# Where the right-hand stack of SBUF tiles begins: an edge of 480 bytes in place of 96, and two constant tiles in the other order

## The chip, the core and the metric

The kernel runs on one core of a Trainium2 chip. The metric is the device time of one execution in microseconds (us), as the median of several runs; smaller is better. The engines are named as the profile names them: PE is TensorE's matrix multiply, PEld its weight load, DVE is VectorE, ACT is ScalarE, POOL is GpSimd and SP is SyncE, which issues the DMA transfers.

## What is computed

Three stages follow each other, all in float32. The first is a chunked linear attention with decay over 4 batches of 8 heads, 768 positions, head size 32 and state size 16. Its result, 3072 tokens of 256 features, passes through two feed-forward layers.

```python
x = attn_out.transpose(0, 2, 1, 3).reshape(B * S, H * D)   # 3072 x 256
h = x @ w_in                                               # 256 -> 2048
g = where(h > 0, h, exp(min(h, 0)) - 1)
x = g @ w_out                                              # 2048 -> 256
g = x @ w_gate; val = x @ w_val                            # 256 -> 1536, twice
out = (g * sigmoid(g) * val) @ w_out2                      # 1536 -> 256
```

## The kernel before

Tokens are worked on in 6 blocks of 512. Features lie on the 128 partitions and the 512 tokens of a block on the free axis, so that a large matmul has a weight of 128x128 as its stationary operand and 128x512 as its moving one. To keep float32 precision with the cheaper type float32r, every operand is split into a high and a low part, and a product is made of three matmuls: high by high, low weight by high, high weight by low (`mm3`, L485 to L493, and `m_c`, L527).

Two feed-forward phases follow each other. In the first, `seq1` runs over 6 blocks of 16 feature tiles f, and one slot of it is `m_a` (6 matmuls that write `h`, L506) and, three slots late, `m_c` (6 matmuls that write `c`, L541). Block 0 is different: its `c` is made by plain float32 matmuls (L535). The attention of the next block's four units is spread among the slots of the current block, so the attention's small matmuls and its work on DVE, ACT and POOL lie beside the feed-forward matmuls. In the second phase a slot (b, f), with 6 blocks of 12 feature tiles, is `s_a` (6 matmuls that write `g` and 6 that write `v`) and, three slots late, `s_c` (6 that write `o`). Each engine runs its instructions in the order in which the program issues them; `m_end` (L544 to L547) empties the accumulators `c` at the end of a block on ACT and DVE.

SBUF is filled from two sides. Tile pools without a side are stacked from low addresses up (the left stack), pools with `side="right"` are stacked from the top of the memory down (the right stack). Each partition's top is at byte 229,344, which is 447 times 512 and 480 more. The right stack begins with a tile named `edge` that nothing reads or writes; after it come `w1p` (the first phase's weights, w1h and w1l), `xp` (its inputs xh and xl), and `stage` (raw weights, e, v). Every tile of the right stack has a size that is a multiple of 512 bytes. With an edge of 24 floats, 96 bytes, every right tile therefore begins 384 bytes past a multiple of 512. On the left, the constant tiles come first: `ident8` (4096 bytes) at byte 16,512, which is 128 past a multiple of 512, then `con` (1408 bytes), also at 128 past one, then `zero_q` (512 bytes) at a multiple of 512. After these `x2` and all further left tiles that a matmul reads begin at a multiple of 512: the split results gh and gl (pool `work`), and in the second phase part of the weights and inputs.

In the second phase the tiles are divided between the two sides by two lines: the weights w2h and w2l of tile f are in the left stack for f below 4 and in the right stack from 4 on, and the block's inputs x2h and x2l are in the left stack for even blocks and in the right one for odd blocks.

```python
pool = ph2["w2l" if f < NHL else "w2h"]      # pair_w2: w2h, w2l (NHL = 4)
pool = ph2["xs" if b % 2 == 0 else "w2h"]    # s_x: x2h, x2l
```

The lower end of the right stack, 132,992 before, lies 384 bytes above the upper end of the left one (132,608) while the attention and the `stage` pool are open.

Of the kernel before, what the change touches and what calls it, by code (L numbers as in the profile page):

```python
# [8 lines left out]
F32 = mybir.dt.float32  # L9
# [38 lines left out]
WARM = 0  # L48
LEAD = 4
CON = 352  # L50
EDGE = 24
VB = 2
OX = 13
NW = 3
# [15 lines left out]
def ssm_mlp_glu_kernel(ctx, tc, a, bcs, xbc, w1, w2, consts, out):  # L70
# [4 lines left out]
    const = ctx.enter_context(tc.tile_pool(name="const", bufs=1))  # L75
    x2p = ctx.enter_context(tc.tile_pool(name="x2p", bufs=1))
    work = ctx.enter_context(tc.tile_pool(name="work", bufs=3))

    ident8 = const.tile([128, H, Q], F32, name="ident8")
    con = const.tile([128, CON], F32, name="con")  # L80
    ident_r, ident, blk_sb, sgn_sb = (con[:, x:y] for x, y in ((0, R), (R, R + Q), (R + Q, R + 2 * Q), (R + 2 * Q, R + 2 * Q + 2)))
    zero_q = const.tile([128, Q], F32, name="zero_q")
    x2_all = x2p.tile([128, 2 * NT], F32, name="x2")
# [1 line left out]

    ctx.enter_context(tc.tile_pool(name="edge", bufs=1, side="right")).tile([128, EDGE], F32, name="edge")
    right = ExitStack()
# [744 lines left out]
```

## Time and profile before

| what | value |
|---|---|
| median of 3 runs | 654.52 us (654.43 to 654.73) |
| the profiled execution's own time | 654.61 us |
| its span, first to last instruction | 652.8 us |
| PE busy | 625.6 us, 96% of the span, 3620 matmuls |
| PEld busy | 490.4 us, 3620 weight loads |
| DVE, ACT, POOL busy | 388.1, 312.2, 315.2 us |
| mean granted TensorE clock | 1.00 of 2.4 GHz |

The span is what the profile sees; the execution's own time is longer by what lies around the first and the last instruction. Busy time of PE is the union of matmuls that overlap in their pipeline, so it says that PE had work, not how fast it went: that is read from the distance between the starts of two matmuls. In the chain of waits, a row such as "1.40 PE o L493 x6" is six matmuls in a row that nothing held up but the one before each.

### The profile page before, as it was taken

The page shows a single profiled execution, that of the slowest core. Times are in us where ns is not written, and L with a number is a line of the kernel's source. Part 1 is how long each engine was busy: PE and PEld are TensorE (multiplying, and loading weights), DVE is VectorE, ACT ScalarE, POOL GpSimd, SP SyncE. Part 2 cuts the span into 40 slices and gives each one's busy share as a digit, 9 for nine tenths or more (in the row PEclk, how much of TensorE's full clock was granted, in tenths as well). Part 3 has the DMA queues.
Part 4 walks back from the last instruction along what each step waited for, and adds up shares of the span by engine and source line. Part 5 has one row for each costly group of instructions (what it writes and reads, how often), then busy time and mean ns, then how long its engine had stood idle before and what let it go on. Part 6 is the DMA issues. An engine that isn't in the chain of part 4 may idle for free.

```text
span 652.8 us, 9659 instructions
## 1 busy us (share of the span) xinstructions
PE 625.6 (96%) x3620; PEld 490.4 (75%) x3620; DVE 388.1 (59%) x580; ACT 312.2 (48%) x562; POOL 315.2 (48%) x263
## 2 busy tenths in 40 slices
PE   2599999999999999999999999999999999999997
PEld 1356667777787778777788888888888888888886
DVE  5869987878887788783574663343343343343332
ACT  2146666666667666666775542322332232332322
POOL 2636657767777577764454332333233333333332
PEclk9999999999999999999999999999999999999999
DMA  6785634454344543410310000000000000000000
GB/s 181 200 286 192 171 111 143 126 151 144 127 133 132 149 133 122 133 33 19 95 50 0 2 1 1 33 0 1 32 1 1 33 1 0 34 0 2 32 1 32
DMA packets 21646, 49.54 MB, mean 76 GB/s; under 512 B 4320, under 2 KB 6496, under 8 KB 21600
## 3 DMA queue, kind: packets, MB, share of 16 engines
q1 hardware_dynamic: 21600, 48.93, 24.1%
q8 instruction: 28, 0.46, 0.3%
q14 instruction: 18, 0.15, 0.1%
HBM read 45.68 MB, written 3.24 MB: 75 GB/s over the span
## 4 chain that ended last, share of the span: by engine, by line
PE 87%; DVE 5%; issue 2%; DMA 2%; ACT 2%; SPq 1%; POOL 0%; POOLq 0%; DVEq 0%; ACTq 0%
PE h L493 18%; PE o L493 15%; PE g L493 15%; PE v L493 15%; PE c L541 14%; PE c L535 4%; DVE E L316 1%; DMA raw<-in_w 1%; PE cb L370 1%; PE y L446 1%; PE y L442 1%; DVE m L521 1%; DVE w2e L140 1%; DMA w2e<-in_xbc 1%; ACT m L515 1%
## 5 line engine op out<-in xcount | busy, mean ns | idle before, releaser
L499 POOL TENSOR_TENSOR gl<-m,gh 128x512 fp32r<-128x512 f32 x152 | 200.1, 1319 | 259.3 <-ACT gh L498 255.5
L613 DVE TENSOR_TENSOR m<-m,g 128x512 f32<-128x512 f32 x72 | 49.5, 688 | 168.5 <-ACT m L608 168.5
L608 ACT ACTIVATE m<-g 128x512 f32<-128x512 f32 x72 | 43.1, 598 | 190.5 <-PE g L493 190.5
L521 DVE SCALAR_TENSOR_TENSOR m<-m,h 128x512 f32<-128x512 f32 x96 | 65.6, 683 | 62.1 <-ACT m L520 62.1
L498 ACT ACTIVATE gh<-m 128x512 fp32r<-128x512 f32 x152 | 94.8, 624 | 1.6 <-DVE m L614 1.0
L515 ACT ACTIVATE m<-h 128x512 f32<-128x512 f32 x96 | 57.1, 595 | 69.1 <-PE h L493 64.5
L493 PE MATMUL h<-xh,w1h 128*128 128x512 f32 x192 | 80.6, 420 | 1.5 <-DVE xl L478 1.0
L493 PE MATMUL h<-xh,w1l 128*128 128x512 f32 x192 | 75.9, 395 | 0.0
L541 PE MATMUL c<-gh,w1h 128*128 128x512 f32 x160 | 63.8, 399 | 1.0 <-DVE x L547 1.0
L541 PE MATMUL c<-gh,w1l 128*128 128x512 f32 x160 | 62.4, 390 | 0.0
L520 ACT ACTIVATE m<-m 128x512 f32<-128x512 f32 x96 | 59.9, 623 | 0.5
L493 PE MATMUL h<-xl,w1h 128*128 128x512 f32 x192 | 59.9, 393 | 0.0
L493 PE MATMUL o<-gl,w2h 128*128 128x512 f32 x144 | 56.7, 394 | 0.0
L493 PE MATMUL g<-x2h,w2h 128*128 128x512 f32 x144 | 56.7, 394 | 0.0
L493 PE MATMUL o<-gh,w2h 128*128 128x512 f32 x144 | 56.6, 393 | 0.0
L493 PE MATMUL o<-gh,w2l 128*128 128x512 f32 x144 | 56.5, 393 | 0.0
L493 PE MATMUL v<-x2h,w2h 128*128 128x512 f32 x144 | 56.5, 392 | 0.0
L493 PE MATMUL g<-x2h,w2l 128*128 128x512 f32 x144 | 56.5, 392 | 0.0
L493 PE MATMUL v<-x2h,w2l 128*128 128x512 f32 x144 | 56.4, 392 | 0.0
L614 DVE TENSOR_TENSOR m<-m,v 128x512 f32<-128x512 f32 x72 | 49.5, 688 | 7.9 <-DVE m L613 0.5
L541 PE MATMUL c<-gl,w1h 128*128 128x512 f32 x160 | 50.4, 396 | 0.0
L493 PEld LDWEIGHTS h<-xh,w1h 128*128 128x128 f32 x192 | 36.4, 190 | 14.4 <-DVE m L521 3.5
(126 smaller groups left out, 1091.3 us busy)
## 6 DMA issues: line engine op xcount, KB each, us to landing
abc<-ac SPq DMA_DIRECT2D x16, 512.0 KB
bcraw<-in_bcs SPq DMA_DIRECT2D x32, 256.0 KB
raw<-in_w SPq DMA_DIRECT2D x15, 512.0 KB
w2e<-in_w SPq DMA_DIRECT2D x12, 512.0 KB
xb<-in_xbc SPq DMA_DIRECT2D x17, 256.0 KB
raw<-in_w SPq DMA_DIRECT2D x12, 256.0 KB
out_y<-yo SPq DMA_DIRECT2D x12, 256.0 KB
abc<-ac SPq DMA_DIRECT2D x8, 128.0 KB
```

The lines of the kernel that those rows point to most:

```text
L140: nc.vector.tensor_scalar(halves(v)[:, :, 0], t["h16"][:, :, 1], 13, None, ALU.logical_shift_right)
L493: nc.tensor.matmul(dst, lhsT=l, rhs=r, start=first and i == 0, stop=last and i == len(ops) - 1, **kw)
L498: nc.scalar.activation(hi, src, AF.Copy)
L499: lo_eng.tensor_tensor(lo, src, hi.bitcast(F32), ALU.subtract)
L515: nc.scalar.activation(m, h, AF.Relu, scale=-1.0)
L520: nc.scalar.activation(m, m, AF.Exp, scale=-1.0)
L521: nc.vector.scalar_tensor_tensor(m, m, -1.0, h, ALU.add, ALU.max)
L535: nc.tensor.matmul(cps[b][m], lhsT=W1["v", f][:, m * 128:(m + 1) * 128], rhs=g, start=f == 0, stop=f == NF1 - 1)
L541: nc.tensor.matmul(cps[b][m], lhsT=w[:, m * 128:(m + 1) * 128], rhs=r, start=f == 0 and w is wh and r is gh, stop=f == NF1 - 1 and r is gl)
L608: nc.scalar.activation(m, pg, AF.Sigmoid)
L613: nc.vector.tensor_tensor(m, m, pg, ALU.mult)
L614: nc.vector.tensor_tensor(m, m, pv, ALU.mult)
```

## The change

The edge grows from 24 to 120 floats (from 96 to 480 bytes), and `con` is allocated before `ident8`. No instruction is added, taken out or reordered.

```diff
-EDGE = 24
+EDGE = 120
...
+    con = const.tile([128, CON], F32, name="con")
     ident8 = const.tile([128, H, Q], F32, name="ident8")
-    con = const.tile([128, CON], F32, name="con")
```

All right tiles move 384 bytes down, and begin at multiples of 512; the lower end of the right stack then meets the upper end of the left one at 132,608. `con` takes byte 16,512 (128 past a multiple of 512, as before) and `ident8` moves to 17,920, a multiple of 512. `zero_q`, `x2` and the rest of the left stack stay where they are, since the sum of the constants is the same.

## Rows read from the trace of the kernel before

**Rows 1.** The page: busy time by engine, TensorE's granted clock in 40 slices, chain by engine.
```profile
PE 625.6 (96%) x3620; PEld 490.4 (75%) x3620; DVE 388.1 (59%) x580; ACT 312.2 (48%) x562; POOL 315.2 (48%) x263
PEclk9999999999999999999999999999999999999999
...
PE 87%; DVE 5%; issue 2%; DMA 2%; ACT 2%; SPq 1%; POOL 0%; POOLq 0%; DVEq 0%; ACTq 0%
```

**Rows 2.** Busy time in stretches: each engine's us and instruction count, then clock, DMA share, GB/s.
```profile
157.00:209.00 52.00, 51.43 (x334) 40.99 (x335) 42.77 (x61) 34.21 (x65) 39.87 (x32) 1.00 0.42 136
...
408.00:457.00 49.00, 49.00 (x216) 40.15 (x215) 18.10 (x26) 14.96 (x26) 14.99 (x13) 1.00 0.03 11
```

**Rows 3.** Waits of PE, from 100 to 346 us: total us, times, longest.
```profile
PE c L541 <- DVE x L547: 1.0, 3, 0.6
```

**Rows 4.** Chain of waits in block 2 of the second phase: start, us, what.
```profile
458.03 1.36 PE g L493 x6
459.39 1.36 PE v L493 x6
460.75 1.37 PE o L493 x6
462.12 1.39 PE g L493 x6
463.51 1.40 PE v L493 x6
```

**Rows 5.** The same view in block 5 of the second phase.
```profile
603.55 1.40 PE g L493 x6
...
628.34 1.38 PE g L493 x6
629.71 1.36 PE v L493 x6
```

**Rows 6.** Timeline of PE in block 4 of the second phase: start, us, instruction.
```profile
558.85 0.39 PE L493 MATMUL v<-x2h,w2h 128*128 128x512 f32 x1
```

**Rows 7.** Timeline of the weight loads at the same place.
```profile
558.85 0.19 PEld L493 LDWEIGHTS v<-x2h,w2l 128*128 128x128 f32 x1
```

**Rows 8.** Timeline of PE: the first matmul of blocks 0, 1 and 2, second phase.
```profile
345.84 0.40 PE L493 MATMUL g<-x2h,w2h 128*128 128x512 f32 x1
...
395.81 0.39 PE L493 MATMUL g<-x2h,w2h 128*128 128x512 f32 x1
...
445.45 0.40 PE L493 MATMUL g<-x2h,w2h 128*128 128x512 f32 x1
```

**Rows 9.** Chain of waits in block 5 of the first phase: one slot.
```profile
316.81 1.39 PE c L541 x6
318.20 1.38 PE h L493 x6
```

**Rows 10.** Chain of waits in block 0: plain float32 matmuls, the last of 15 rows.
```profile
98.70 1.72 PE c L535 x4
```

**Rows 11.** Chain of waits at the end of a block of the first phase: first and last piece off PE.
```profile
248.31 0.60 ACT m L515
...
261.21 0.61 DVE x L547
```

**Rows 12.** Scans on DVE, by shape: line, operation, count, busy us, mean ns.
```profile
L316 DVE TENSOR_TENSOR_SCAN E<-abc,ident 128x1024 f32<-128x1024 f32 x16 | 36.2, 2265 | 0.1
...
L316 DVE TENSOR_TENSOR_SCAN E<-abc,x 128x512 f32<-128x512 f32 x5 | 6.0, 1205 | 0.7 <-ACT x L647 0.7
...
L334 DVE TENSOR_TENSOR_SCAN P<-ahn,zero_q 128x128 f32<-128x128 f32 x14 | 5.7, 407 | 0.0
```

**Rows 13.** Chain of waits: transfers on it, into the right stack and into the left.
```profile
5.46 4.56 DMA raw<-in_w
19.60 4.23 DMA w2e<-in_xbc
...
145.37 3.78 DMA raw<-in_w
```

## The prediction

> **What bounds the kernel now.** I read the page first. PE is busy for 625.6 of 652.8 us at a granted clock that stands at the top digit in every slice, and the chain of waits lies on PE for 87% [rows 1]. So the end is set by how fast PE goes through its matmuls, and the clock has nothing left to give. The busy times by stretch say where this holds. In a block of the second phase PE is busy for all 49.00 us while DVE, ACT and POOL work 15 to 18 us; in a block of the first phase PE still has 51.43 of 52 us, but DVE has 42.77 [rows 2]. PE's own waits there are few: 1.0 us in three places, all for the DVE copy that empties an accumulator at a block's end [rows 3]. PE is thus the bound, with little slack only around those three places.
>
> Busy time doesn't tell what a matmul costs, so I next read the chain of waits for groups of six matmuls, which all have the same shape (128x128 by 128x512) and no wait among them. They don't take the same time. In block 2 of the second phase the groups g, v, o take 1.36, 1.36, 1.37 us and the next g and v 1.39 and 1.40 [rows 4]; in block 5 it goes the other way round, 1.40 for g of an early tile and 1.38 and 1.36 for g and v of a later one [rows 5]. The code says what differs. Block 2 has its inputs on the left; its weights are on the left up to f = 3, on the right after that, and the change from 1.37 to 1.39 falls on g of f = 4. Block 5 has its inputs on the right, and its rows change at f = 4 in the opposite sense. Fast are left with left and right with right; slow is one of each. Tile number, block and position in the slot are excluded by this reversal.
>
> The timelines show why two operands can meet at all: a matmul (558.85 us) and the load of the next weight (also 558.85 us) begin together, and the load runs for 0.19 us beside it [rows 6, 7]. So PE reads two tiles at once. Left tiles begin at 0 modulo 512, right ones at 384. The rows fit this reading: when the moving operand and the weight loaded beside it begin at the same place modulo 512, six matmuls take about 1.36 us (227 ns each), otherwise about 1.40 (233 ns). Whatever the reason in the memory, the rows hold at both places, 0 with 0 and 384 with 384.
>
> **The edge.** It makes all right tiles begin at 0, so every pair becomes an equal one. No queue gets or loses an instruction; what moves is the pitch of the matmuls.
>
> Second phase: blocks start at 345.84, 395.81 and 445.45 [rows 8], so an even block takes 49.97 us, an odd one 49.64; the next three repeat this within 0.02. A block is 12 slots of three groups. With three groups at 1.36, a slot is 4.08 and a block 48.96. (The run of equal pairs from 458.03 to 462.12 took 4.09 [rows 4], but beside its last matmul a right-hand weight is already loading.) The gain is 1.01 for an even block and 0.68 for an odd one, three of each: 5.1 us. At 4.09 it would be 12 x 4.09 = 49.08 a block and 4.4 us in all; I keep that as the low end.
>
> First phase: a slot is 1.39 for c (moving operand left, weights right) and 1.38 for h (both right) [rows 9], 2.77 together; 5 blocks of 16 such slots make 80. That h isn't at 1.36, although its pair is equal, needs a choice. The first g behind an unequal o is also slower than what follows it (1.38, and 1.36 for the v after it [rows 5]), so I read 1.38 as the trace of the unequal c before it: PE needs a few matmuls to fall into step. With c equal, h should fall too. The attention's small matmuls break in some four times a block, though, so I take the 4.09 of the mixed run: two thirds of it, 2.727 a slot, 0.043 less than now, times 80: 3.4 us. Ends: 2.72 a slot (4.0 us), or c falls to h's 1.38 and h stays (0.01 x 80 = 0.8 us).
>
> What is lost of it: at three block ends the chain leaves PE (from 248.31 to the end of the DVE copy at 261.82 in one of them [rows 11], 13.6 us through ACT and DVE), and PE waits for that copy already [rows 3]. A faster PE arrives earlier and waits longer. In 13.6 us at 1.6% (0.043 of 2.77) that is 0.21 us each, 0.65 for three; it is the work that is late next. Its ends are nothing lost, and all of the first phase's gain.
>
> Block 0's plain float32 matmuls are 1.72 for four in all 15 of the chain's rows, of which one is shown [rows 10], though a third of their weights lies on the right: no gain, no loss. The 45 us of start before them hang on transfers and on the attention; nothing there gets faster.
>
> **The transfers into and out of right tiles.** Their count and size stay; their start in a partition moves from 384 to 0. The trace doesn't show that case. A 512 KB load into a right tile took 4.56 us on the chain at the start, a 256 KB load into a left one 4.23, and one such right load stands on the chain again later, 3.78 us [rows 13]. The nearest bound is the whole difference of the first two, 0.33 us either way for each of the two that are on the chain. I take nothing: their times follow the queue rather than the place.
>
> **The constants' order.** `con` keeps its place modulo 512, `ident8` goes from 128 to 0. It is read only by DVE's 16 large scans. Two scans that read at 0 give a slope: (1205 - 407) / (512 - 128) = 2.078 ns per element, 141 ns fixed, thus 2269 ns for 1024 elements; those that read `ident8` at 128 take 2265 [rows 12]. The place makes 4 ns, 0.06 us over all 16, on an engine that is not the bound. I take nothing; ends are plus and minus 0.06.
>
> **The sum.** 5.1 + 3.4 - 0.65 = 7.85 us off the profiled execution's 654.61 (its span 652.8 and 1.8 around it, which the change doesn't touch): 646.8. The median of the runs is 0.09 below the profiled one, so 646.7.
>
> **A page that speaks against it.** The Trainium skill, page "SBUF — State Buffer", section "Who interferes with whom", gives PE two independent read ports, one for the moving operand and one for the weight load, and says that PE never waits on anyone. By it the place of a tile would change nothing and the time would stay at 654.5. The trace does not agree: 1.36 against 1.40 us for the same six matmuls, turning with the side of the tiles. It counts as a rival below.
>
> **The rivals.**
> *The first phase gives nothing back.* DVE has 42.77 of 52 us there [rows 2], and its queue is in order: E's scan, the copy and the m's of the feed-forward stand behind each other. If its waits take what PE gains, or h and c keep their pace, only the second phase counts: 5.1, thus 649.4. For it: three waits are there already [rows 3]. Against: they are 1.0 us in 200, and DVE is fed by PE for most of a block, so it moves up with it.
> *Places don't matter.* The rows' two paces come from something else that goes with the sides, such as distance in memory or the neighbours of a tile. Then the shift does nothing: 654.5. Against: the reversal at f = 4, and that all twelve weight tiles go by their side alone, wherever in it they lie.
> *A crowded place: slower.* gh, gl, m and x2, which ACT, DVE and POOL write and read while PE reads, lie at 0 as well; right with right (at 384) may be fast because it keeps away from them. If at 0 every group goes at 1.40, a slot of the second phase takes 4.20 and a block 50.40: 0.43 and 0.76 more, 3.6 for six. A first-phase slot takes 2.80, 0.03 more, 2.4 for 80. Together 660.5. The point from which it decides is a mean above today's: 1.384 us a group (99.61 us for two blocks of 72 groups in all). Against: the run at 458.03 has everything on the left, at 0, and is as fast as any [rows 4].
>
> **How the numbers follow.** The forecast has 0.74, the first rival 0.17, places don't matter 0.04, slower 0.05. Everything at its best, 5.1 + 4.0 and nothing lost, gives 645.4; the low ends, 4.4 + 0.8 - 0.65 = 4.55, give 650.0. The range 645.2 to 650.0 holds the forecast and the first rival. Faster by over 0.2% (1.3 us, about what a measurement of this kernel tells from no change): 0.91; within 0.2%: 0.04; slower: 0.05.
>
> **What would show it.** In the chain of the changed kernel every g, v and o group should read 1.36 or 1.37 in all blocks, even and odd blocks should both take 49.0 us, and c and h should read 1.36 to 1.38, with a slot at 2.72 to 2.73. The wait of c for the copy of x should grow from 1.0 to about 1.6 us. Float32 groups should stay at 1.72 and the large scan at 2265 ns. Wrong would be groups at 1.39 or 1.40 that remain for f from 4 on, paces that differ between even and odd blocks, or a new wait of PE for ACT or DVE of more than 1 us.

## The result

The changed kernel takes 646.92 us (median of 4 runs, 646.43 to 647.97) against 654.47 for the kernel before (654.24 to 654.73): a ratio of 0.9887, 95% interval 0.9870 to 0.9904. The forecast was 646.7. The profiled execution took 647.97, of which its span is 646.2; it is the slowest of the four because of its start, as is shown below. One execution of all, 897.09 us at a granted clock of 0.669 in the run with the right stack at 64, is left out of the times below; all others ran at 0.999 or 1.000.

The page of the changed kernel: busy time by engine, granted clock, chain by engine.

```profile
PE 618.0 (96%) x3620; PEld 490.6 (76%) x3620; DVE 387.7 (60%) x580; ACT 312.2 (48%) x562; POOL 314.6 (49%) x263
PEclk9999999999999999999999999999999999999999
...
PE 86%; DVE 6%; DMA 3%; issue 2%; POOL 1%; ACT 1%; SPq 1%; POOLq 0%; DVEq 0%; ACTq 0%
```

Instruction counts are those of [rows 1], and so is the clock; PE's busy time has fallen by 7.6 us, that of every other engine has moved by at most 0.6. PE is still the bound.

The chain of waits at the place of [rows 4], block 2 of the second phase around f = 4: start, us, what.

```profile
454.74 1.36 PE g L493 x6
456.10 1.36 PE v L493 x6
457.46 1.36 PE o L493 x6
458.82 1.36 PE g L493 x6
```

The step from 1.37 to 1.39 at f = 4 is gone. An early tile of block 5, which took 1.40 in [rows 5]:

```profile
601.62 1.36 PE g L493 x6
```

The timeline of PE: the first matmul of blocks 0, 1 and 2 of the second phase, as in [rows 8].

```profile
344.42 0.39 PE L493 MATMUL g<-x2h,w2h 128*128 128x512 f32 x1
...
393.38 0.39 PE L493 MATMUL g<-x2h,w2h 128*128 128x512 f32 x1
...
442.34 0.39 PE L493 MATMUL g<-x2h,w2h 128*128 128x512 f32 x1
```

Even and odd blocks now both take 48.96 us, where they took 49.97 and 49.64; the starts of blocks 3, 4 and 5 repeat this. The first phase, one slot without attention (c, then h), as in [rows 9]:

```profile
312.87 1.36 PE c L541 x6
314.23 1.36 PE h L493 x6
```

h has fallen along with c, though h's own pair had been equal before. The float32 groups of block 0 are where they were [rows 10]:

```profile
96.42 1.72 PE c L535 x4
```

One wait grew. PE's waits from 100 to 346 us, the row of [rows 3]:

```profile
PE c L541 <- DVE x L547: 1.5, 3, 0.7
```

The chain at the block end of [rows 11] still leaves PE for 13.5 us, now with a transfer of raw weights on it:

```profile
247.82 0.60 ACT m L515
...
249.34 3.54 DMA raw<-in_w
...
260.70 0.61 DVE x L547
...
261.36 1.21 PE c L541 x4
```

Where the time came from can be added up from starts. Each fence has the first h of block 0, which ends the start, and the first h of block 1; blocks 1 to 5 last from there to the first g of the second phase (345.84 in [rows 8], 344.42 above). The kernel before:

```profile
35.33 0.79 PE L493 MATMUL h<-xh,w1h 128*128 128x512 f32 x1 [1.00 <-DVE xl L478]
...
93.67 0.79 PE L493 MATMUL h<-xh,w1h 128*128 128x512 f32 x1
```

The changed kernel:

```profile
36.08 0.80 PE L493 MATMUL h<-xh,w1h 128*128 128x512 f32 x1 [1.00 <-DVE xl L478]
...
94.47 0.79 PE L493 MATMUL h<-xh,w1h 128*128 128x512 f32 x1
```

Blocks 1 to 5 of the first phase took 345.84 - 93.67 = 252.17 us before and 344.42 - 94.47 = 249.95 after: 2.22 less. The second phase gave 1.01 for each even block, 0.68 for each of the first two odd ones and 0.83 for the last block with the end behind it: from its first g to the end of the span it took 307.0 us before and 301.8 after, 5.2 less. The start, up to block 0, was 0.75 us longer in this execution, and block 0 itself equal (58.34 and 58.39). 5.2 + 2.2 - 0.8 = 6.6, all of the 6.6 us between the two profiled executions. The longer start belongs to this execution: the spans of the same kernel's other three are 644.7, 645.0 and 645.3 us, 0.9 to 1.5 below the profiled one. Over all kernels of this text the first h comes between 34.7 and 36.4 us in the profiles. The three with the edge of 480 bytes are the latest of them (36.0 to 36.4), so profiles alone would not rule out an effect; but the changed kernel's median (646.92) agrees with that of the kernel whose large matmuls have all their tiles at 128 (646.98, below), whose first h came at 35.2.

### The profile page after: what moved, and what is told of

Same layout as the page of the kernel before. It is cut to its first block, busy times and chain, and to the rows that moved or that the text cites. A ratio compares the mean times of both kernels' runs of the same rounds, so it can differ in the third digit from the quotient of the medians.

```text
span 646.2 us, 9659 instructions
## 1 busy us (share of the span) xinstructions
PE 618.0 (96%) x3620; PEld 490.6 (76%) x3620; DVE 387.7 (60%) x580; ACT 312.2 (48%) x562; POOL 314.6 (49%) x263
## 4 chain that ended last, share of the span: by engine, by line
PE 86%; DVE 6%; DMA 3%; issue 2%; POOL 1%; ACT 1%; SPq 1%; POOLq 0%; DVEq 0%; ACTq 0%
PE h L493 18%; PE o L493 15%; PE g L493 15%; PE v L493 15%; PE c L541 14%; PE c L535 4%; DMA raw<-in_w 2%; DVE E L316 1%; PE cb L370 1%; PE y L446 1%; DMA x<-ac 1%; PE y L442 1%; DVE w2e L143 1%; DVE w2e L140 1%; DVE m L521 1%
```

## The experiments

**The edge alone.**

```diff
-EDGE = 24
+EDGE = 120
```

> Edge of 480 bytes alone, constants in the old order. Theory (the edge does all of it: every matmul's moving operand and the weight loaded beside it begin at the same place modulo 512): 646.9 us, from 646.4 to 648.0, all groups of the second phase at 1.36 us. Rival (the constants' order has a part, by ident8 at 0 instead of 128): up to 0.5 us above the changed kernel, 647.4 or more, with the large scans of L316 slower than 2265 ns.

Measured: 647.52 us (646.91 to 648.34), ratio 0.9896 (0.9881 to 0.9911), an interval that overlaps the changed kernel's. Its chain in block 2:

```profile
457.80 1.36 PE o L493 x6
459.16 1.36 PE g L493 x6
460.52 1.36 PE v L493 x6
```

Both phases take as long as in the changed kernel (blocks 1 to 5 of the first 249.98 and 249.95 us). The large scan takes 2265 ns here as in [rows 12]; in the changed kernel:

```profile
L316 DVE TENSOR_TENSOR_SCAN E<-abc,ident 128x1024 f32<-128x1024 f32 x16 | 36.2, 2264 | 0.1
```

By the medians the rival's 647.4 or more would hold; by the profile it doesn't, since neither the scans nor the phases differ. The 0.6 us lie within what one kernel's executions scatter (646.43 to 647.97 for the changed one).

**The constants' order alone.**

```diff
-EDGE = 120
+EDGE = 24
```

(against the changed kernel)

> Constants in the new order alone, edge of 96 bytes. Theory: nothing moves, 654.5 us within 0.5, blocks of the second phase 49.97 and 49.64 us as before. Rival (the order has a part): 653.5 to 654.0.

Measured: 654.43 us (653.96 to 655.13), ratio 0.9997 (0.9988 to 1.0007): nothing. Its chain keeps the step at f = 4:

```profile
460.11 1.37 PE o L493 x6
461.47 1.39 PE g L493 x6
```

**Equal places, none of them 0.**

```diff
-CON = 352
-EDGE = 120
+CON = 384
+EDGE = 88
```

> Left stack moved up 128 bytes (constant tile of 384 floats) and right stack begun at 128 past a multiple of 512 (edge of 352 bytes): no tile that a large matmul reads begins at 0, but all begin at the same place. Theory (equal places modulo 512 count, not place 0): 646.9 us, from 646.3 to 648.0, groups at 1.36 us, blocks 48.96. Rival (place 0 is what helps): groups at 1.39 to 1.40 us, blocks of 50.0 to 50.4, 654 to 660 us.

Measured: 646.98 us (646.42 to 647.15), ratio 0.9886 (0.9871 to 0.9900). Block 2, behind f = 4:

```profile
460.66 1.36 PE o L493 x6
462.02 1.36 PE g L493 x6
```

This is the changed kernel's time with no tile that a large matmul reads at 0. That tiles lie at 0 isn't what helps; that they lie alike is.

**Left at 0, right at 256.**

```diff
-EDGE = 120
+EDGE = 56
```

> Right stack begun at 256 past a multiple of 512 (edge of 224 bytes), left at 0. Theory (what counts repeats every 512 bytes): the unequal pairs stay slow, groups near 1.40 us in even blocks from f = 4 on, 653 to 657 us. Rival (it repeats every 256 bytes): 646.9 us with 1.36 everywhere. Were it finer, 128, the kernel before would have had no slow group.

Measured: 647.47 us (646.74 to 648.17), ratio 0.9894 (0.9880 to 0.9909). Block 2, behind f = 4, where every g and v has its input on the left and its weight on the right:

```profile
460.31 1.36 PE o L493 x6
461.67 1.36 PE g L493 x6
463.02 1.36 PE v L493 x6
```

My theory fell in one point: tiles 256 bytes apart are as fast as equal ones, so the pattern repeats every 256 bytes and not every 512. It is no finer than that, since 128 and 384 apart were slow in the kernel before.

**Left at 0, right at 32.**

```diff
-EDGE = 120
+EDGE = 112
```

> Right stack begun at 32 past a multiple of 512, left at 0, so that pairs of a left and a right tile stand 32 or 480 apart modulo 512. Known so far: 0 and 256 apart cost 1.36 us a group, 128 and 384 apart 1.39 to 1.40. Theory A (only pairs that stand a multiple of 256 apart are fast): groups of left with right near 1.40 us, 653 to 657 us. Rival B (the cost grows with the distance within 256, up to its half): groups between 1.36 and 1.38, 647 to 650 us. Rival C (32 is within one unit of the memory and counts as equal): 646.9.

Measured: 656.76 us (656.10 to 657.36), ratio 1.0032 (1.0020 to 1.0045): slower than before. Block 2, around f = 4:

```profile
460.20 1.36 PE v L493 x6
461.56 1.37 PE o L493 x6
462.93 1.40 PE g L493 x6
```

**Left at 0, right at 64.**

```diff
-EDGE = 120
+EDGE = 104
```

> Right stack begun at 64 past a multiple of 512, left at 0: pairs stand 64 or 448 apart. Theory A (only multiples of 256 are fast): near 1.40 us a group of left with right, 653 to 657 us. Rival B (the cost grows with the distance): more than at 32 apart and less than at 128, groups near 1.38, 649 to 652 us. Rival C (units of 128 bytes or coarser): as at 32 apart, 646.9.

Measured: 656.26 us (655.68 to 657.55), ratio 1.0028 (1.0017 to 1.0039). Block 2, around f = 4:

```profile
461.37 1.36 PE o L493 x6
462.73 1.40 PE g L493 x6
```

Both are theory A by their times and by these rows. Pairs 32, 64, 128, 384, 448 and 480 bytes apart are slow, none by a cost that grows with the distance, and pairs 0 and 256 apart are fast. So a tile need not be far off to be slow: 32 bytes cost a little more than the 384 of the kernel before. But the distance isn't everything. With the right stack at 64, block 5 has its inputs on the right; v of f = 0 and of f = 1, both 448 apart, and v of f = 4, an equal pair:

```profile
597.63 1.37 PE v L493 x6
...
601.80 1.40 PE v L493 x6
...
614.33 1.38 PE v L493 x6
```

Block 3 repeats this within 0.01. What makes one pair at 448 nearly fast and another slow, no run shows.

**One equal pair made unequal.** In the kernel before, a pad between the first phase's weights and its inputs:

```diff
+    right.enter_context(tc.tile_pool(name="pad", bufs=1, side="right")).tile([128, 96], F32, name="pad")
     xp = right.enter_context(tc.tile_pool(name="xp", bufs=2, side="right"))
```

> The kernel before with a pad of 384 bytes between the first phase's weights and its inputs: weights stay at 384, xh and xl begin at 0 (the staging tiles after them too). Theory (equal places count): h, until now an equal pair, becomes unequal and goes from 1.38 to about 1.40 us, c stays at 1.39 to 1.40, the second phase stays at 49.97 and 49.64 us a block: 80 slots by 0.02 to 0.04 us more, 655.5 to 658 us. Rival (a moving operand at 0 is what helps): h at 1.36, 80 x 0.02 = 1.6 us less, 653.

Measured: 655.82 us (655.35 to 656.71), ratio 1.0022 (1.0012 to 1.0031). Its chain in block 5 of the first phase (line numbers are one higher for the added line):

```profile
316.53 1.40 PE h L494 x6
317.92 1.40 PE c L542 x6
```

The input h reads was brought to 0 and got slower, 1.38 to 1.40, since its weight stayed at 384. The second phase stayed as before. This separates the pair from the place in the first phase too.

**What eats the first phase's gain.** The changed kernel with both copies at a block's end on ACT:

```diff
-        nc.vector.tensor_copy(x2[b][:, 1, :], c[1])
+        nc.scalar.activation(x2[b][:, 1, :], c[1], AF.Copy)
```

> The changed kernel with the second accumulator's copy at a block's end on ACT instead of DVE. Theory (part of the first phase's gain is lost in PE's wait for this copy behind DVE's scan, 1.5 us in three places): the wait for DVE goes and PE resumes earlier, 645.2 to 646.3 us. Rival (the wait only changes its releaser, since the chain before it runs through ACT and DVE anyway, or ACT's second copy of 0.6 us delays the next gh): 646.5 to 647.5 us, a wait of c for ACT in its place.

Measured: 644.45 us (644.17 to 645.10), ratio 0.9845 (0.9830 to 0.9859): the fastest kernel of this study, 2.5 us below the changed one, more than either side expected. PE's wait for the copy is gone, and no other takes its place from 100 to 340 us. Its chain at the block end stays on PE:

```profile
251.27 1.36 PE c L541 x6
...
260.00 1.36 PE h L493 x6
```

The first h of block 1 and the first g of the second phase:

```profile
94.38 0.79 PE L493 MATMUL h<-xh,w1h 128*128 128x512 f32 x1
...
341.51 0.39 PE L493 MATMUL g<-x2h,w2h 128*128 128x512 f32 x1
```

Blocks 1 to 5 take 247.13 us, 2.82 less than in the changed kernel, of which 1.5 is the wait that the profile had put down to the copy. Most of the rest shows in the starts of the changed kernel's matmuls, here at the ends of blocks 1 and 4:

```profile
156.90 0.39 PE L541 MATMUL c<-gh,w1l 128*128 128x512 f32 x1
158.01 0.50 PE L541 MATMUL c<-gh,w1h 128*128 128x512 f32 x1 [0.72 <-DVE x L547]
...
309.91 0.39 PE L541 MATMUL c<-gh,w1l 128*128 128x512 f32 x1
310.30 0.50 PE L541 MATMUL c<-gh,w1h 128*128 128x512 f32 x1
```

From start to start the first two are 1.11 us apart, where such a step takes 0.23 without a wait: 0.88 is lost, and the waits count only 0.72 of it, because the row of the matmul before lasts 0.39 us, 0.16 longer than a step. At 309.91 a step of 0.39 us is a loss that counts as no wait at all. Held against this run matmul by matmul, the changed kernel loses 0.86, 0.71, 0.71 and 0.31 us at the ends of blocks 1 to 4, 2.6 of the 2.82. Another 0.22 goes before one group of the attention's matmuls (cb, 113.96); why the copy bears on that, no run shows.

**The same on the kernel before.**

> The kernel before, edge of 96 bytes, with both accumulator copies on ACT as in the run that gained 2.5 us on the changed kernel. Theory (the faster PE arrives earlier at the copy, so the copy's wait eats 0.5 us or more of what the edge gives the first phase): the copies give less here, 1.3 to 2.0 us, 652.5 to 653.2, and the distance to the changed kernel with both copies on ACT is 8.0 us or more, above the 7.5 that the edge gave alone. Rival (copies and edge don't meet): 2.5 us here too, 652.0, distance 7.5.

Measured: 652.39 us (652.02 to 653.18), ratio 0.9969 (0.9957 to 0.9982). The same two starts:

```profile
93.69 0.79 PE L493 MATMUL h<-xh,w1h 128*128 128x512 f32 x1
...
343.66 0.40 PE L493 MATMUL g<-x2h,w2h 128*128 128x512 f32 x1
```

249.97 us for blocks 1 to 5. Without the wait for DVE the edge gives the first phase 249.97 - 247.13 = 2.84 us, with it 2.22: the wait eats 0.62. By the medians the edge gives 652.39 - 644.45 = 7.9 us without the wait and 7.55 with it. That is the sign that the theory wanted and just short of its numbers (652.5 at the least, a distance of 8.0), but the intervals of the ratios (about 1 us wide each way) don't separate it from the rival. The 0.62 comes from profiles: the two runs with both copies on ACT have one each, but the 2.22 is repeated. With an edge of 96 bytes and either order of the constants the blocks took 252.17 and 252.05 us, and the four kernels with all pairs 0 or 256 apart took 249.90 to 249.98.

## Why the prediction was right

*The reading of the two paces* held: the edge does all of it (edge alone 647.52, order alone 654.43), and PE's pace goes by how the tile that streams and the tile that is loaded beside it lie to each other. Wrong in it was "at the same place modulo 512": pairs 256 bytes apart are as fast as equal ones. It had no part in the sum, since the change makes all pairs equal, and the trace of before, with distances of 0, 128 and 384 only, could not show it.

*The sum*, 7.85 us: the medians give 7.55, the two phases in the profiles 5.2 + 2.2 = 7.4. The excess lies in the first phase, whose net term of 3.4 - 0.65 = 2.75 us measured 2.2.

*The second phase*, 5.1 us, measured 5.2: 48.96 a block was predicted, and 48.96 measured in each of the five blocks that another one follows. The choice of 1.36 instead of the mixed run's 4.09 a slot was the right one: beside that run's last matmul a right-hand weight had been loading.

*The first phase*, 3.4 us: measured 2.84 where no wait interferes. This is the term that was mis-sized. The slot fell further than taken (2.72 where nothing breaks in, not 2.727), but 80 such slots was too many. The h group right behind the attention's small matmuls, 16 times in blocks 1 to 5, gained nothing. One of them in the chain of the kernel before, then of the changed one:

```profile
230.87 1.58 PE h L493 x6
...
230.59 1.58 PE h L493 x6
```

That h at 1.38 was only the trace of the unequal c before it fits two runs: h falls to 1.36 when c becomes equal, and rises to 1.40, not 1.38, when it is made unequal itself.

*What is lost at block ends*, 0.65 us: measured 0.62. The wait for the copy grew from 1.0 to 1.5 us, where 1.6 was expected, and taking the copy off DVE gave the time back. (The 13.6 us of the working are 13.5 by the ends that it names; that changes nothing.) Too low was the reading that PE's waits cost 1.0 us before: taking the copy off DVE gave blocks 1 to 5 of the kernel before 252.17 - 249.97 = 2.2 us.

*Nothing from the constants' order, float32 groups and transfers*: the scan took 2264 against 2265 ns [rows 12], and the float32 groups stayed at 1.72. What the transfers into right tiles gain or lose can't be told from the scatter of the start; that they change nothing is not shown.

*The rivals.* "The first phase gives nothing back" was wrong by 2.2 us. "Places don't matter" fell with the first experiment; the Trainium skill's statement on the page "SBUF — State Buffer", section "Who interferes with whom", that PE's two read ports are independent and PE never waits on anyone, does not fit this kernel: the same six matmuls take 1.36 or 1.40 us when nothing but the places of tiles is changed. "A crowded place" fell twice, as all at 0 and all at 128 give the same time.

## What to carry to other kernels

Where a profile's matmuls of one shape have two paces, compare where the moving operand and the next weight begin in their partition: here a difference that was not a multiple of 256 bytes cost up to 7 ns on a matmul of 227 (1.40 against 1.36 us for six). A few bytes of padding at the foot of a stack can set it, and everything allocated on top moves with it. When PE gets faster, look at once for the place where it now arrives too early; a small copy on the busiest other engine held back 2.0 us before the change and 2.5 after it. And read what a wait costs from the starts of the instructions around it, not from the idle time alone.

## What the runs showed of the hardware

The fast pace is exact: 1.36 us for six matmuls, 48.96 for 216, is 226.7 ns each, 544 cycles at 2.4 GHz for 512 columns. The Trainium skill, page "TensorE: Matmul & The Clock Gate", section "Back-to-back issue gap", gives N / 2.4 + 2.5 ns for the gap of an isolated matmul, about 216 for 512 columns, and about 131 ns for a sustained stream of weight loads and matmuls. This kernel is such a stream, in float32r and at the clock's higher level throughout, and no run of it held a pace below 226.7. The slow pace depends on more than the distance: an equal pair that follows an unequal one stays slow for some matmuls (h at 1.38 before, 1.36 after, its own pair equal in both), and pairs at the same 448 bytes read 1.37 and 1.40. What in the memory repeats every 256 bytes no run shows, nor whether distances finer than 32 bytes would differ.
